# A recurrent attention chain and the linear attention behind it: order of the last attention, and of the hand-over between the two

## The chip, the cores and the metric

The kernel runs on one core of a Trainium2 chip. The metric is the device time of one execution in microseconds (us); the time of a kernel is the median of its timed runs. A separate execution is recorded by the hardware profiler, instruction by instruction, and all rows shown below come from such executions. Engines are called PE (TensorE matmul), PEld (TensorE weight load), DVE (VectorE), ACT (ScalarE), POOL (GpSimd) and SP (SyncE, which here only issues DMAs). A name such as L1049 is a line of the kernel.

## The reference

The input has 2048 rows of 640 numbers in bf16. Four layers are applied, A, B, A, B, each as `x = x + layer(layernorm(x))`.

Layer A is recurrent. The rows are cut into 64 segments of 32, and 8 memory rows are carried from segment to segment:

```
for s in range(64):
    h = concat([mem, xs])                       # 8 + 32 rows
    q, k, v = h @ Wq, h @ Wk, h @ Wv            # 32 heads of 192
    p = softmax(mask(q k^T / sqrt(192)))
    o = (p v) @ Wo
    mem = o[:8]; outs.append(o[8:])
```

A segment can't begin before the 8 memory rows of the one before it are known.

Layer B is a linear attention with 32 heads of 20. For q and k it makes the features `[softmax(x w_phi), softmax(-x w_phi)]`, sums `kv = phi_k^T v` and `z = sum(phi_k)` over all rows, and returns `(phi_q kv) / (phi_q z + 1e-6) @ wo`.

## The kernel before

**The chain of layer A** (`A_chain`). The chain projects the 8 memory rows and 24 of a segment's 32 own rows. The keys, queries and values of the last 8 rows are made ahead for all segments (`A_pre`) and fetched segment by segment (`extra_kq`, `extra_v`); their scores and outputs are made in the chain with the others. The 32 heads are worked in four rounds of eight. The rounds run upwards in even segments and downwards in odd ones, so that weights which are still in the local memory are used again; the others are loaded anew each time by SP.

In a round the chain projects Q and K (L972), copies and transposes them (L982, L987, L990 to L992), adds the extra columns on GpSimd (L948 to L951), makes masked scores (L1009, L1014), weights E by `exp` (`weigh`, L1067), their sums (`sums`, L1081) and the normalised weights (`normalise`, L1086 to L1088), projects V (L972), and applies the weights (`attend`, L1022). The output product W with `Wo` (`wo_round`, L1049) is written as 12 steps for each round, each with four products in 32-column tiles of TensorE. Software writes the order of all engines out by hand inside the chain (`manual_schedule`, L908), one instruction stream per engine, in which no instruction passes another. At the end of a segment the order on TensorE is: steps 0 to 3 of the second round's `wo_round`, last scores, steps 4 and 5, third attention, steps 6 and 7, sums of the last round, steps 8 to 11, the third round's `wo_round`, a few products that only keep TensorE occupied (`keep_busy`, L1056), fourth attention, the fourth `wo_round`, more such products. VectorE then transposes W (L1195, L1196) into the next segment's memory columns.

**Stored outputs.** The attention outputs of the last 8 rows of each segment (columns 64 to 80 of the accumulators `ps_o`) aren't multiplied with `Wo` in the chain. `keep_tail` (L1035, L1037, L1038) copies them into `otb`, which has two buffers, and `store_tail` (L1042, on GpSimd's queue) stores them into a DRAM tensor `otb_d`, one store per round, 512 in the kernel.

**The hand-over to layer B** (`post_steps`, and the part of `layer_B` from L485 on). The stored outputs are brought back in four groups of 16 segments: `fetch` (L1210, SP's queue) loads a group, `spread` reorders it by four copies (L87 on VectorE, L89 on ScalarE), and `multiply` makes 48 pairs of products with `Wo` (L1228, L1229), evicts them (L1231, L1232) and stores them beside the chain's rows. In the first layer B, 32 steps that multiply two weight matrices into one (`fuse`: L166, L393) are called between the pairs of the third and fourth group. `norm_rows` (L352) adds the attention's rows to x (L356, GpSimd) and normalises them (L222 to L244); `turn_rows` (L361) transposes them. The arena of local memory is used by both layers, so a load of layer B waits for the last reader of layer A.

Outside `manual_schedule` a planner in the software orders the instructions of each engine by the times that it expects; `tc.issue_after(i)` says that what follows is queued behind instruction i on that engine, and adds no wait. The planner may also put instructions of layer B among the last ones of the chain.

**Keys, values and normalisers of layer B.** For each 512 rows, `keys_values` makes exponentials of the keys (L424), their sums and reciprocals (L426, L428), copies the reciprocals into the value tile (L433, GpSimd), multiplies the values with them (L437) and adds up `kv` (L443). After the fourth group, each of the twelve parts of `kv` is masked (L529), and its column of z is copied into two places (L534 to L537).

Of the kernel before, what the change touches and what calls it, by code (L numbers as in the profile page):

```python
# [20 lines left out]
FILL = {0: 86, 2: 78}  # L21
# [94 lines left out]
class Kernel:  # L116
# [131 lines left out]
    def layer_B(self, x_dram, at_dram, xout_dram, xnext_dram, li, bp, post):  # L248
# [42 lines left out]
        with tc.tile_pool(name=f"B{li}_kv", bufs=1, space=bass.MemoryType.PSUM, reuse_waits="tile") as kvp, \  # L291
# [121 lines left out]
            def keys_values(g, xnT):  # L413
                VS = DH * (512 // DH)

# [15 lines left out]
                def values(b, ek, rk):  # L431
                    vr = vrs.next().rearrange("p (s h f) -> p s h f", s=2, h=H)
                    nc.gpsimd.tensor_copy(out=vr[:, :, :, DH], in_=rk[:])  # L433
# [50 lines left out]

            with tc.issue_after(self.last_load.ins):  # L485
                load_rows(0)
            fetch, spread, multiply = post
            ot = [fetch(tb) for tb in range(2)]
            ow = [spread(tb, ot[tb]) for tb in range(2)]
            ot += [fetch(tb) for tb in range(2, 4)]  # L490
            for j in (1, 2, 0):
                src = self.B_wqkv.rearrange("(k p) n -> p k n", p=P) if j == 2 or self.fused_d is None else self.fused_d
                nc.sync.dma_start(out=wqkv[:, :, D * j:D * j + D], in_=src[:, :, D * j:D * j + D])
            multiply(0, ow[0], kv_ps[0], side_bank("ps_post"))
            ow.append(spread(2, ot[2]))
            rows = [norm_rows(b) for b in range(4)]
            multiply(1, ow[1], kv_ps[1], side_bank("ps_post"))
            ow.append(spread(3, ot[3]))
# [4 lines left out]
            multiply(2, ow[2], kv_ps[0], side_bank("ps_post"), side)  # L503
            first_xnT = new_xnT()
            for b in range(4):
                turned = turn_rows(b, rows[b], first_xnT)
            multiply(3, ow[3], kv_ps[1], side_bank("ps_post"), side)
            assert not side
            waiting = None
            for g in range(NG):  # L510
                if g == 0:
                    xnT = first_xnT
                elif g == 1:
                    with tc.issue_after(turned.ins):
                        xnT = norm_T(g)
                else:
                    xnT = norm_T(g)
# [7 lines left out]
            for sg in range(2):  # L525
                for c in range(NC_):
# [4 lines left out]
                    for u in range(2):  # L531
                        z = zm[0:mc, sg, c, 32 * u + HC * c:32 * u + HC * c + nh]
                        if sg == 0:
                            nc.vector.scalar_tensor_tensor(out=z, in0=o[:, :, DH], scalar=1e-6, in1=blk[0:mc, 0:nh], op0=ALU.add,  # L534
                                                           op1=ALU.mult)
                        else:
                            nc.vector.tensor_tensor(out=z, in0=o[:, :, DH], in1=blk[0:mc, 0:nh], op=ALU.mult)  # L537
# [734 lines left out]
```

## Time and profile before

| | us |
|---|---|
| median of the timed runs (three) | 3646.74 |
| lowest and highest of them | 3642.9 and 3680.07 |
| the profiled execution | 3628.7 |
| its span, first to last instruction | 3627.0 |
| chain of the first layer A, about | 140 to 1557 |
| first hand-over, to the first keys | 1557 to 1627 |
| second layer A's chain ends | 3370 |
| second hand-over, to the first keys | 3370 to 3426 |

How the rows are to be read. In a timeline, a row has the start, the duration, the engine, the line, the operation, what it writes and reads, the shapes, how many were merged, and in square brackets how long the engine had stood idle and what ended that. In a list of waits, a row has the engine and the instruction that waited, the instruction it waited for, the sum in us, how often, and the longest. In a table by stretches, a row has the stretch, its length, the busy time of PE, PEld, DVE, ACT and POOL with numbers of instructions, the granted TensorE clock (1 is full), the busy share of the DMA engines and their GB/s. Matmuls are pipelined and their ends are modelled, so the distance of two starts tells more than a duration. The granted clock over the whole span was 0.990.

### The profile page before, as it was taken

The page shows a single profiled execution, that of the slowest core. Times are in us where ns is not written, and L with a number is a line of the kernel's source. Part 1 is how long each engine was busy: PE and PEld are TensorE (multiplying, and loading weights), DVE is VectorE, ACT ScalarE, POOL GpSimd, SP SyncE. Part 2 cuts the span into 40 slices and gives each one's busy share as a digit, 9 for nine tenths or more (in the row PEclk, how much of TensorE's full clock was granted, in tenths as well). Part 3 has the DMA queues.
Part 4 walks back from the last instruction along what each step waited for, and adds up shares of the span by engine and source line. Part 5 has one row for each costly group of instructions (what it writes and reads, how often), then busy time and mean ns, then how long its engine had stood idle before and what let it go on. Part 6 is the DMA issues. An engine that isn't in the chain of part 4 may idle for free.

```text
span 3627.0 us, 168472 instructions
## 1 busy us (share of the span) xinstructions
PE 3484.6 (96%) x70944; PEld 2279.2 (63%) x71398; DVE 2332.7 (64%) x6336; ACT 2040.4 (56%) x5233; POOL 1598.2 (44%) x4181
## 2 busy tenths in 40 slices
PE   9989999999999999989999899999999999999899
PEld 7756666666666666655367566666666666666453
DVE  5556666666666666646643566766666676766465
ACT  3356666666566656645432565666666666666463
POOL 3445555555555555531122455555545555555300
PEclk9999999999999999999999999999999999999999
DMA  9988887888788878870387887888888788888600
GB/s 302 338 286 290 284 290 271 285 293 287 270 283 291 290 271 282 293 228 8 130 270 208 287 291 270 291 292 283 282 288 294 274 292 295 281 286 292 214 1 30
DMA packets 533265, 933.32 MB, mean 257 GB/s; under 512 B 141066, under 2 KB 300442, under 8 KB 532506
## 3 DMA queue, kind: packets, MB, share of 16 engines
q1 hardware_dynamic: 431098, 821.50, 64.3%
q0 software_dynamic: 67744, 87.80, 8.0%
q10 hardware_dynamic: 33664, 13.24, 1.4%
q8 instruction: 557, 9.13, 1.0%
q14 instruction: 202, 1.65, 0.1%
HBM read 852.43 MB, written 73.73 MB: 255 GB/s over the span
## 4 chain that ended last, share of the span: by engine, by line
PE 57%; DMA 19%; DVE 7%; issue 7%; ACT 5%; POOL 3%; PEld 2%; SPq 0%; POOLq 0%; DVEq 0%; ACTq 0%
PE ps_qk L972 17%; DMA arena<-wo_rows 7%; PE ps_w L1049 7%; PE ps_v L972 6%; DMA Vp<-vb 5%; PE ps_o L1022 4%; PE ps_pre L863 3%; DMA arena<-in_A_Wv_dram 3%; PE ps_s L1014 3%; DVE hT L928 2%; PE ps_s L1081 2%; PE ps_s L1009 2%; PE ps_pre L887 2%; PE ps_wo L410 2%; PE ps_idle L1056 1%
## 5 line engine op out<-in xcount | busy, mean ns | idle before, releaser
L972 PEld LDWEIGHTS <-hT 128*32 128x32 bf16 x30720 | 753.5, 96 | 453.5 <-issue 29.5
L972 PE MATMUL ps_qk<-arena,hT 128*32 128x384 bf16 x20480 | 998.6, 327 | 11.2 <-DMA arena<-in_A_Wq_dram 2.2
L982 ACT ACTIVATE raw<-ps_qk 128x384 bf16<-128x384 f32 x1024 | 503.2, 491 | 377.0 <-PE ps_s L1081 250.7
L955 POOL DMA_DIRECT2D Vp<-vb x512 | 259.2, 506 | 629.6 <-PE ps_o L1022 467.1
L972 PE MATMUL ps_v<-arena,hT 128*32 128x384 bf16 x10240 | 515.6, 328 | 15.7 <-DMA arena<-in_A_Wv_dram 15.1
L1049 PE MATMUL ps_w<-arena,OT 128*32 128x160 bf16 x18432 | 471.3, 235 | 16.0 <-DMA arena<-wo_rows 15.0
L987 DVE STREAM_TRANSPOSE KT<-raw 128x384 bf16<-128x384 bf16 x512 | 296.1, 578 | 192.1 <-ACT raw L982 188.2
L1049 PEld LDWEIGHTS <-OT 128*32 128x32 bf16 x18432 | 321.1, 96 | 116.5 <-issue 23.6
L990 DVE STREAM_TRANSPOSE QT<-raw 128x256 bf16<-128x256 bf16 x512 | 227.9, 445 | 238.3 <-ACT raw L982 196.5
L943 POOL DMA_DIRECT2D kqb<-kqb x512 | 292.1, 571 | 174.0 <-POOL KT L951 147.0
L1003 DVE CAST Vp<-ps_v 64x384 bf16<-64x384 f32 x512 | 286.1, 559 | 107.3 <-ACT Vp L1001 95.7
L1088 DVE TENSOR_TENSOR E<-E,ps_s 80x320 bf16<-80x320 bf16 x512 | 247.3, 483 | 164.6 <-ACT ps_s L1087 164.2
L1042 POOL DMA_DIRECT2D otb<-otb x512 | 283.9, 554 | 129.6 <-DVE otb L1038 110.8
L1001 ACT ACTIVATE Vp<-ps_v 64x384 bf16<-64x384 f32 x512 | 245.2, 479 | 128.4 <-PE ps_v L972 128.3
L1067 ACT ACTIVATE E<-ps_s 80x320 bf16<-80x320 f32 x512 | 221.9, 433 | 84.8 <-PE ps_s L1014 43.7
L1022 PEld LDWEIGHTS <-Vp 80*128 80x128 bf16 x4096 | 183.5, 99 | 128.1 <-issue 80.2
L1022 PE MATMUL ps_o<-E,Vp 80*128 80x80 bf16 x4096 | 235.6, 203 | 26.3 <-DMA Vp<-vb 10.9
L1014 PE MATMUL ps_s<-QT,KT 128*80 128x80 bf16 (+1 forms) x3072 | 234.0, 213 | 12.4 <-DVE KT L987 10.6
L936 ACT ACTIVATE Vp<-ps_w 32x160 bf16<-32x160 f32 x512 | 150.8, 295 | 167.6 <-DVE wt L1195 154.0
L1086 ACT ACTIVATE ps_s<-ps_s 80x320 f32<-80x320 f32 x512 | 215.3, 420 | 41.6 <-PE ps_s L1081 41.6
L948 POOL COPY QT<-kqb 128x64 bf16<-128x64 bf16 x512 | 125.4, 245 | 252.6 <-PE ps_s L1014 244.7
L1014 PEld LDWEIGHTS <-KT 128*80 128x80 bf16 x3072 | 201.9, 119 | 39.1 <-issue 30.4
(155 smaller groups left out, 5453.8 us busy)
## 6 DMA issues: line engine op xcount, KB each, us to landing
arena<-wo_rows SPq DMA_DIRECT2D x792, 320.0 KB, 6.8
arena<-in_A_Wq_dram SPq DMA_DIRECT2D x427, 384.0 KB, 4.5
arena<-in_A_Wv_dram SPq DMA_DIRECT2D x427, 384.0 KB, 6.4
arena<-in_A_Wk_dram SPq DMA_DIRECT2D x768, 192.0 KB, 4.8
kqb<-kqb POOLq DMA_DIRECT2D x512, 48.0 KB, 5.1
arena<-in_A_Wk_dram SPq DMA_DIRECT2D x43, 384.0 KB, 6.8
vb<-arena POOLq DMA_DIRECT2D x128, 112.0 KB, 5.9
Vp<-vb POOLq DMA_DIRECT2D x512, 28.0 KB, 4.8
```

What stands on the lines that cost most here:

```text
L943: nc.gpsimd.dma_start(out=kqb[:], in_=self.kqb_d[s, :, r, :])
L955: nc.gpsimd.dma_start(out=Vs[n % 2][64:80, :], in_=self.vb_d[s, r].rearrange("g t f -> (g t) f"))
L972: nc.tensor.matmul(o[32 * g:32 * g + 32, 0:384], lhsT=hT[:, b, :], rhs=rhs, start=(i == 0), stop=(i == KC - 1), tile_position=(0, 32 * g), ...
L982: nc.scalar.activation(out=raw[:], in_=ps[:, 0:384], func=ACT.Copy)
L987: nc.vector.transpose(out=KT[:, :, 0:64], in_=raw[:, :].rearrange("p (c j) -> p c j", j=64))
L1001: nc.scalar.activation(out=o, in_=i, func=ACT.Copy)
L1003: nc.vector.tensor_copy(out=o, in_=i)
L1014: nc.tensor.matmul(S[0:80, c0:c0 + 80 * (q1 - q0)], lhsT=KT[:, 3 * x + i, :], rhs=QT[:, x, q0:q1, :], start=False, stop=(x == 1 and i == 2 ...
L1022: nc.tensor.matmul(O[x][:, 80 * i:80 * i + 80], lhsT=Vs[n % 2][0:80, 448 * x + k:448 * x + k + 128], rhs=E[0:80, 160 * x + 80 * e:160 * x ...
L1042: nc.gpsimd.dma_start(out=self.otb_d[s, :, 96 * r:96 * r + 96], in_=otb[:, :, :].rearrange("p c t -> p (c t)"))
L1049: nc.tensor.matmul(W[32 * g:32 * g + 32, 0:160], lhsT=OT[:, c, q:q + 32], rhs=w[:, 640 * i + 160 * g:640 * i + 160 * g + 160], start=(firs ...
L1088: nc.vector.tensor_tensor(out=E[0:80, 0:320], in0=E[0:80, 0:320], in1=rc, op=ALU.mult)
```

## The change

It has six parts.

1. In each segment of the chain, the third attention comes right behind the last scores. Steps 4 and 5 of the earlier `wo_round` move behind it, and steps 6 to 11 all come behind the sums.
2. `otb_d` gets the partition as its outermost dimension: a store writes 192 B in each of 128 places 48 KB apart, and a fetch reads 12 KB from each in place of sixteen times 768 B.
3. The first two groups' fetches are issued in the chain's last segment, one before and one behind the load of the last output weights; the first group is spread there too, behind the fourth attention, by two copies on VectorE and two on ScalarE. The second group's copies are queued behind the chain's last copies on their engines.
4. Keys' and queries' weights of layer B are loaded ahead of x's rows and of the values' weights. The weight products move from the third and fourth group's products to the second and third's. The first four layer norms are queued on VectorE and ScalarE behind the third group's eviction, and their transposes go between the products of the fourth group.
5. The reciprocals of the first 512 rows are copied by VectorE; GpSimd copies the others as before.
6. The column of z is written to its two places by one instruction in place of two: 12 in place of 24 in each layer B. One more filling weight load (79 in place of 78) stands at the second chain's start.

```diff
-FILL = {0: 86, 2: 78}
+FILL = {0: 86, 2: 79}
...
-                    nc.gpsimd.tensor_copy(out=vr[:, :, :, DH], in_=rk[:])
+                    (nc.gpsimd if g else nc.vector).tensor_copy(out=vr[:, :, :, DH], in_=rk[:])
...
+            fetch, spread, multiply = post
+            ot, ow = self.first_tails
             with tc.issue_after(self.last_load.ins):
+                for j in (1, 0):
+                    src = self.B_wqkv.rearrange("(k p) n -> p k n", p=P) if self.fused_d is None else self.fused_d
+                    last = nc.sync.dma_start(out=wqkv[:, :, D * j:D * j + D], in_=src[:, :, D * j:D * j + D])
+            with tc.issue_after(last.ins):
                 load_rows(0)
-            fetch, spread, multiply = post
-            ot = [fetch(tb) for tb in range(2)]
-            ow = [spread(tb, ot[tb]) for tb in range(2)]
+            with tc.issue_after(self.chain_end[0].ins), tc.issue_after(self.chain_end[1].ins):
+                ow.append(spread(1, ot[1]))
             ot += [fetch(tb) for tb in range(2, 4)]
-            for j in (1, 2, 0):
-                src = self.B_wqkv.rearrange("(k p) n -> p k n", p=P) if j == 2 or self.fused_d is None else self.fused_d
-                nc.sync.dma_start(out=wqkv[:, :, D * j:D * j + D], in_=src[:, :, D * j:D * j + D])
-            multiply(0, ow[0], kv_ps[0], side_bank("ps_post"))
+            with tc.issue_after(last.ins):
+                nc.sync.dma_start(out=wqkv[:, :, 2 * D:3 * D],
+                                  in_=self.B_wqkv.rearrange("(k p) n -> p k n", p=P)[:, :, 2 * D:3 * D])
+            multiply(0, ow[0], kv_ps[0], side_bank("ps_post"), {})
             ow.append(spread(2, ot[2]))
-            rows = [norm_rows(b) for b in range(4)]
-            multiply(1, ow[1], kv_ps[1], side_bank("ps_post"))
-            ow.append(spread(3, ot[3]))
             side = []
             if self.fused_d is None:
                 self.fused_d = self.dram.tile([P, KC, 2 * D], BF16, name="fused")
                 side = fuse(1) + fuse(0)
-            multiply(2, ow[2], kv_ps[0], side_bank("ps_post"), side)
+            between = [{3 * i + 2: f for i, f in enumerate(part)} for part in (side[:16], side[16:])]
+            multiply(1, ow[1], kv_ps[1], side_bank("ps_post"), between[0])
+            ow.append(spread(3, ot[3]))
+            done = multiply(2, ow[2], kv_ps[0], side_bank("ps_post"), between[1])
+            with tc.issue_after(done[0].ins), tc.issue_after(done[1].ins):
+                rows = [norm_rows(b) for b in range(4)]
             first_xnT = new_xnT()
-            for b in range(4):
-                turned = turn_rows(b, rows[b], first_xnT)
-            multiply(3, ow[3], kv_ps[1], side_bank("ps_post"), side)
+            turned = []
+            multiply(3, ow[3], kv_ps[1], side_bank("ps_post"),
+                     {35 + 4 * b: lambda b=b: turned.append(turn_rows(b, rows[b], first_xnT)) for b in range(4)})
...
-                    with tc.issue_after(turned.ins):
+                    with tc.issue_after(turned[-1].ins):
...
-                    for u in range(2):
-                        z = zm[0:mc, sg, c, 32 * u + HC * c:32 * u + HC * c + nh]
...
+                    z = zm[0:mc, sg, c, :].rearrange("p (u h) -> p u h", u=2)[:, :, HC * c:HC * c + nh]
+                    zs, own = bcast_mid(o[:, :, DH], 2), bcast_mid(blk[0:mc, 0:nh], 2)
...
-        self.otb_d = dram.tile([NSEG, P, 384], BF16, name=f"otb{li}")
+        self.otb_d = dram.tile([P, NSEG, 384], BF16, name=f"otb{li}")
...
                             if s == NSEG - 1:
+                                tails = [self.fetch_tails(0, low)]
                                 load_wo(3, low[:, 0:7680])
+                                tails.append(self.fetch_tails(1, low))
...
                 S, E = weigh(True)
-                wo_round(W, order[L - 2], OT1, False, False, range(4, 6))
                 OT, o = attend(Ep, L - 1, KT[:, :, 0:64])
...
-                wo_round(W, order[L - 2], OT1, False, False, range(6, 8))
+                wo_round(W, order[L - 2], OT1, False, False, range(4, 6))
                 sums(S, E)
-                wo_round(W, order[L - 2], OT1, False, False, range(8, 12))
+                wo_round(W, order[L - 2], OT1, False, False, range(6, 12))
...
                 OT, o = attend(E, L)
                 tails_after(L)
+                if s == NSEG - 1:
+                    self.first_tails = tails, [self.spread_tails(0, tails[0], low, "vvss")]
...
+    def fetch_tails(self, tb, low):
+        o = 7680 + 12288 * (tb % 2)
+        ot = low[:, o:o + 6144].rearrange("p (s f) -> p s f", f=384)
+        self.nc.sync.dma_start(out=ot, in_=self.otb_d[:, 16 * tb:16 * tb + 16, :])
+        return ot
+
+    def spread_tails(self, tb, ot, low, engines="vsvs"):
+        o = 7680 + 12288 * (tb % 2)
+        ow = low[:, o + 6144:o + 12288].rearrange("p (c q) -> p c q", q=P)
+        for k in range(4):
+            self.ev.copy(out=ow[:, 12 * k:12 * k + 12, :].rearrange("p c (s t) -> p c s t", t=8),
+                         in_=ot[:, :, 96 * k:96 * k + 96].rearrange("p s (c t) -> p c s t", t=8), eng=engines[k])
+        return ow
```

`chain_end` holds the chain's last copy on VectorE (of `keep_tail`) and on ScalarE (of `keep_rows`).

## The prediction

> **What bounds the kernel now.** I read the busy shares first, then TensorE's waits in the two stretches where an attention layer hands over to a linear layer, then the timeline of those stretches, then one ordinary segment.
>
> ```profile
> PE 3484.6 (96%) x70944; PEld 2279.2 (63%) x71398; DVE 2332.7 (64%) x6336; ACT 2040.4 (56%) x5233; POOL 1598.2 (44%) x4181
> ```
>
> TensorE is busy 96% of the span, so only two things can shorten the run: its idle time (3627.0 - 3484.6 = 142 us), and stretches in which it runs slowly. TensorE's waits from 1540 to 1700 us, the first handover:
>
> ```profile
> PE ps_s L1014 <- DVE KT L987: 5.1, 1, 5.1
> PE ps_f L393 <- ACT arena L89: 4.1, 2, 2.9
> PE kv L443 <- POOL arena L433: 3.5, 1, 3.5
> PE ps_v L410 <- ACT arena L424: 2.4, 3, 1.1
> PE ps_f L393 <- DVE arena L87: 1.3, 1, 1.3
> ```
>
> The second handover (3340 us on) has the first again with 5.6 us, the third with 3.5, and neither `ps_f` row, since the weight products are made once. Where the first wait comes from, in the timeline:
>
> ```profile
> 1536.78 0.38 SPq L1210 DMA_DIRECT2D arena<-otb  x1
> ...
> 1548.40 0.56 DVE L87 COPY arena<-arena 128x1536 bf16<-128x1536 bf16 x1 [5.23 <-issue]
> ...
> 1548.88 0.57 DVE L987 STREAM_TRANSPOSE KT<-raw 128x384 bf16<-128x384 bf16 x1
> ...
> 1549.59 0.72 PE L1014 MATMUL ps_s<-QT,KT 128*80 128x80 bf16 x6 [5.09 <-DVE KT L987]
> ```
>
> The copy L87 is the first spreading copy of the linear layer. The planner queued it on VectorE ahead of the K transpose that the last segment's last scores need; its fetch (L1210), issued at 1536.78, has landed only at 1548.4. The chain stands still behind it. What that does to the clock (each row of this table by stretches ends with granted clock, DMA share and GB/s):
>
> ```profile
> 1545.00:1550.00 5.00, 0.41 (x5) 0.44 (x6) 1.49 (x3) 1.57 (x2) 3.79 (x6) 0.89 1.06 362
> 1550.00:1555.00 5.00, 4.90 (x101) 3.64 (x100) 2.20 (x6) 3.27 (x7) 0.58 (x1) 0.50 1.06 348
> ```
>
> After 5 us without work the clock is 0.50 in the next 5. The DMA engines are full (1.06), which matters below.
>
> **The change, part by part.**
>
> *Spreading of the first stored outputs at a fixed place.* It now stands behind the last attention. The chain's stop goes: 5.1 and 5.6 us. With it goes the slow clock: from the scores to the segment's end takes 7.9 us (1549.6 to 1557.5) and 7.5 us (3362.9 to 3370.4), against 5.8 in an ordinary segment (1011.0 to 1017.3 less a DMA wait of 0.5), so 2.1 and 1.7. Together 7.2 and 7.3. What is late next is the fetch itself. It is now queued behind the six loads of the last output weights. From 1538.8 us, the first of those loads: 6 x 0.33 = 1.97 MB, then 1.57 MB of outputs, and some 0.6 MB still in flight, 4.1 MB at the 355 GB/s of the two rows above: 11.7 us, and about 1 for the last piece to be told, so 1551.5; the first copy (0.56) ends at 1552.1. The chain without its stop ends 5.8 us after 1544.6, at 1550.4. TensorE then waits 1.7 us: the gain is 1557.5 - 1552.2 = 5.3; 3370.4 - 3365 = 5.4 at the second. Both ends: 3 (an SP queue that stops) and 7.2 (the transfer is in time, since 128 pieces of 12 KB may move quicker than 2048 of 768 B). I take 5.3: it follows from rows.
> ScalarE's two spreading copies (1.48 each) now stand ahead of its last keep_tail and keep_rows copies. Nothing on the path waits for those: their rows are needed by the fourth fetch, 30 us later. Without that cover (if the first product's accumulator still held the last outputs) it would cost 3 us per handover, contained in the low end.
>
> *Order of SP's queue.* Two fetches, then keys' and queries' weights, then rows, then the other fetches, then the values' weights. No instruction of SP issues faster or slower; bytes are the same 13 MB in 40 us. The second fetch lands at about 1561 (another 3.5 MB), while the first product runs to 1565 (48 x 0.272 = 13.1 us by the rows of L1228/L1229): hidden. The third lands near 1571 and is needed at 1582: hidden for itself, but see the first rival.
>
> *Weight products in the second and third product instead of the third and fourth; layer norms behind them.* The waits of the `ps_f` rows, 4.1 + 1.3 = 5.4 us, come from evictions queued behind the norms of the first rows; both engines have no norms in front of them now. Once only. New: the same evictions can be queued behind the third spreading, which waits for its fetch. Ends 0 and 4 us; I take 1.5, since five transposes and four banks run ahead of it. The norms start when the third product is evicted. Chain of a row block from the timeline: 0.9 statistics, 0.4 moments, 0.5 ScalarE, 0.3 VectorE, 0.9 apply: 3 us, next blocks 1.4 apart, and the first transposition comes 35 x 0.272 = 9.5 us into the last product: hidden. In the second layer 0.9 + 0.7 us of waits (`ps_x`, `ps_post`) go. Norms of the next 512 rows (6 us VectorE, 6 us ScalarE) move under the first key blocks, where each has about a third free.
>
> *The reciprocals' copy on VectorE for the first 512 rows.*
>
> ```profile
> 1635.24 2.74 POOL L356 TENSOR_TENSOR arena<-arena 128x640 bf16<-128x640 bf16 x2 [5.80 <-DMA arena<-attn]
> 1637.93 0.46 POOL L433 CAST arena<-rk 128x64 bf16<-128x64 f32 x1
> ...
> 1638.44 0.58 PE L443 MATMUL kv<-arena 128*120 128x126 bf16 x4 [3.53 <-POOL arena L433]
> ```
>
> The copy stands behind 2.74 us of additions on GpSimd. VectorE's products were there from 1634.8: 3.5 us go, and the clock of 0.55 in 1640 to 1645 (5 x 0.45 = 2.2). Against that four copies on VectorE of some 0.15 to 0.2 each (nearest row: a 128x48 cast, 0.2) and the norms that moved here. Ends 2 and 6 per layer; I take 4.
>
> *Twelve normaliser steps fewer.* 24 of 0.1 us in each layer are 12; TensorE waits for none of them (0.5 us of other waits there). Zero; ends 0 and 1.
>
> *Third attention right behind the last scores, 128 times.* An ordinary segment:
>
> ```profile
> 2364.51 0.48 DVE L1088 TENSOR_TENSOR E<-E,ps_s 80x320 bf16<-80x320 bf16 x1 [0.18 <-ACT ps_s L1087]
> 2364.52 0.45 PE L1014 MATMUL ps_s<-QT,KT 128*80 128x80 bf16 x6
> 2364.90 0.12 PEld L1049 LDWEIGHTS <-OT 128*32 128x32 bf16 x8
> ...
> 2365.16 0.46 PE L1022 MATMUL ps_o<-E,Vp 80*128 80x80 bf16 x8
> ...
> 2365.80 0.33 PE L1081 MATMUL ps_s<-E,ones_blk 80*80 80x320 bf16 x1
> ```
>
> Eight output products (L1049, 32-column tiles) lie between scores and attention. The last score starts at 2364.77, so they cost 0.38 there; placed with the others of their kind they cost 2 x 0.07. The Trainium skill (TensorEngine Tiling (Array Packing), Key Properties) says that changing the tiling mode drains TensorE; one pair of changes disappears. By that rule alone a segment gets 0.38 - 0.04 - 0.14 = 0.20 shorter, 26 us in 128. The rows say otherwise: the third attention's weights E end at 2364.99, so it can start only 0.05 later, at 2365.04 instead of 2365.16, and TensorE idles 0.23 there. The sums come 0.12 earlier, the two moved steps are then in the way again, and the fourth attention can start 0.09 earlier where it waits for its own E. Over the 128 segments of the trace that is so in 33 (the fourth attention starts within 0.075 of E's end); in the rest a transfer of V rows lands later and the gain is lost there. 33 x 0.09 = 3 us; ends 0 and 11 (all 128).
>
> *Stored outputs with the partition outermost.* Each store is still 128 pieces of 192 B, now 48 KB apart. The skill (DMA: Bandwidth & Descriptors, Latency and other measured facts) warns of large row pitches in HBM: 207 GB/s at 512 KB, about half at 4 MB. It speaks against the change, but the trace's loads of Wq have a pitch of 60 KB and bring 384 KB in 4.5 us; a pitch below 512 KB in the rule and near 60 KB in the trace: zero. The other end is the third rival.
>
> **Sum**, against the profiled execution (3628.7 us; span 3627.0): first handover 5.3 + 5.4 - 1.5 + 4 = 13.2, second 5.4 + 1.6 + 4 = 11.0, chain 3: 27 us, giving 3601 there. The timed runs' median is 3646.74, 18 above that execution; the difference is not the change's, so 3646.7 - 27 = 3620.
>
> **Rivals.**
> - *The waits come back in another place* (0.22): SP stops between the loads, the first product waits 3 us more, evictions wait behind the third spreading. Gain 12 to 18: 3631. For it: DMA full from 1540 to 1580. Against it: the bytes fit.
> - *The drain rule holds in full* (0.08), because E comes earlier than I read: 3620 - 23 = 3597. Against it: E's end sits 0.22 behind the last score in most segments.
> - *The tail stores get slow* (0.09), on the other side. Two buffers of `otb` are in turn; ScalarE already waits for the older store:
>
> ```profile
> ACT Vp L936 <- DVE wt L1195: 154.0, 123, 2.3
> ACT otb L1037 <- DMA otb<-otb: 87.9, 110, 1.7
> ```
>
>  Behind that copy ScalarE has 1.25 us to spare (154.0/123). A store takes 4.7 us in the median; from 6 on every further us is paid 128 times. At 6.4: 0.45 x 128 = 58, less 27: 3678; at 7, 3750.
> - *The fetch is not freed* (0.08): if the new layout makes the first fetch wait for the latest stores, the chain's later stores queue behind it, some 10 us a layer: 3640.
> My forecast, 3604 to 3632, has 0.53.
>
> **How the numbers follow.** 3599 to 3648 holds the forecast, the first, the fourth and part of the second. One per cent, 36 us, is about what a measurement of this kernel can tell from no change. Faster by more: 0.22 (the second rival, the forecast's lower edge and the unknown ends up together). Slower by more: 0.07 of the third. The rest is within.
>
> **What would show it.** Right: no wait of L1014 for L987 at the handovers; the first product some 5 us earlier after a short wait for the spreading; no `ps_f` wait of over 1 us; no wait of `kv` for GpSimd; the clock not at 0.50 after the chain; in a segment a TensorE gap of 0.2 ahead of the third attention. Wrong: L1037 or L1035 waiting longer for stores, an eviction of `ps_t` queued behind a spreading copy, or a segment period that moved by over 0.1 us.

## The result, and the profile after

The changed kernel took 3619.61 us in the median of nine runs (3614.55 to 3631.28), the kernel before 3645.82 beside it: a ratio of 0.9922, 95% interval 0.9894 to 0.995, 26.2 us less. On a second chip it was 3601.32 against 3627.89, 0.9918 (0.9898 to 0.9938), 26.6 us less. The profiled execution took 3619.27 us, its span was 3617.5.

Lines have moved: the scores are now L1019, the attention L1027, `wo_round` L1054, the sums L1086, the weights E L1093, the fetch L1213, the first of each pair of products L1243, `keep_tail` on ScalarE L1042, the reciprocals' copy L432, `kv` L442. The busy shares of the page of after:

```profile
PE 3470.1 (96%) x70978; PEld 2278.5 (63%) x71399; DVE 2329.5 (64%) x6320; ACT 2030.9 (56%) x5233; POOL 1592.2 (44%) x4173
```

TensorE's waits from 1525 to 1660 us, the first hand-over (sum, how often, longest):

```profile
PE kv L1243 <- DVE arena L87: 3.8, 1, 3.8
PE ps_v L410 <- ACT arena L423: 3.0, 3, 1.3
PE kv L442 <- DVE arena L436: 1.4, 2, 0.9
PE ps_w L1054 <- issue: 0.3, 1, 0.3
```

Three of the old rows are gone: the scores' wait for the K transpose (5.1), both waits of `ps_f` (5.4) and the wait of `kv` for GpSimd (3.5). One is new: the first product waits 3.8 us for the first spreading copy, and 4.6 at the second hand-over. Where it comes from, in the timeline:

```profile
1538.97 0.32 SPq L1213 DMA_DIRECT2D arena<-otb  x1
1539.35 5.15 SPq L687 DMA_DIRECT2D arena<-wo_rows  x6
...
1544.44 1.15 PE L1054 MATMUL ps_w<-arena,OT 128*32 128x160 bf16 x48
...
1549.40 1.03 DVE L87 COPY arena<-arena 128x1536 bf16<-128x1536 bf16 x2 [4.99 <-DMA arena<-otb]
...
1550.02 0.61 PE L1243 MATMUL kv<-arena 128*128 128x512 bf16 x1 [3.83 <-DVE arena L87]
```

The fetch, issued at 1538.97, lands 10.4 us later. The chain's last product has ended at 1545.6, and behind a few filling products TensorE has nothing else to do. In the table by stretches the clock behind that wait is 0.69, and 0.56 at the second hand-over (third number from the end), and each pair of products takes 0.53 us in place of 0.27:

```profile
1545.00:1550.00 5.00, 1.19 (x33) 0.78 (x23) 0.60 (x2) 0.54 (x1) 0.38 (x1) 0.97 1.00 333
1550.00:1555.00 5.00, 4.98 (x25) 2.52 (x26) 0.54 (x2) 3.59 (x7) 1.15 (x2) 0.69 1.07 420
...
3365.00:3370.00 5.00, 2.44 (x9) 1.17 (x10) 1.14 (x3) 3.03 (x4) 0.00 (x0) 0.56 1.06 402
```

The trace places the slow clock more closely. It is 0.50 from 1549.7 for 3.4 us and from 3365.6 for 6.8 us. In before it is 0.50 for 6.8 us at the end of each of the four stops (two at the scores, two at `kv`): from 1548.9, 1637.7, 3361.4 and 3436.5.

An ordinary segment now, in the timeline:

```profile
2352.29 0.48 DVE L1093 TENSOR_TENSOR E<-E,ps_s 80x320 bf16<-80x320 bf16 x1 [0.18 <-ACT ps_s L1092]
2352.29 0.45 PE L1019 MATMUL ps_s<-QT,KT 128*80 128x80 bf16 x6
...
2352.82 0.45 PE L1027 MATMUL ps_o<-E,Vp 80*128 80x80 bf16 x8
2353.20 0.32 PE L1054 MATMUL ps_w<-arena,OT 128*32 128x160 bf16 x8
2353.45 0.33 PE L1086 MATMUL ps_s<-E,ones_blk 80*80 80x320 bf16 x1
```

The third attention starts 0.05 behind the end of its weights E. Over 126 segments it starts, in the median, 0.271 us behind the start of the last score (before: 0.384), the last sums 0.900 (1.027). But the distance of two segments (last sums to last sums) has a median of 21.20 us, and 21.15 before; the second profiles have 21.12 and 21.10. TensorE's waits over the whole run show where the 0.1 us went. Before, and then after:

```profile
PE ps_w L1049 <- DMA arena<-wo_rows: 15.0, 25, 4.2
PE ps_w L1049 <- issue: 11.7, 30, 0.9
```

```profile
PE ps_w L1054 <- DMA arena<-wo_rows: 25.3, 52, 6.2
...
PE ps_w L1054 <- issue: 17.4, 32, 1.4
```

The stores of the tails have not changed: they land 4.8 us after their issue (4.7 before). ScalarE waits longer for them, 103.7 us in place of 87.9, which was to be a sign of being wrong. It is not the layout's: the second profiles have 97.6 and 95.4, and the run e1 below, with the old layout, has 105.4.

Stage by stage, two profiles of each kernel say more than one. The second profile of before comes from the run `e0_before_again`, that of after from `e10_after_again`. All times count from the last sums of the chain's last segment but one, so that the length of the chain falls out; us.

| up to | before, 2 profiles | after, 2 profiles | mean gain |
|---|---|---|---|
| first hand-over: first product | 33.2, 31.8 | 29.9, 30.3 | 2.4 |
| first keys | 102.8, 102.5 | 95.4, 94.4 | 7.7 |
| last `kv` | 215.7, 214.8 | 204.5, 203.5 | 11.2 |
| second chain's first sums | 475.6, 477.7 | 467.1, 467.1 | 9.5 |
| second hand-over: first product | 33.2, 33.0 | 31.5, 29.4 | 2.6 |
| first keys | 88.1, 92.4 | 87.8, 85.0 | 3.9 |
| last `kv` | 202.3, 203.9 | 196.7, 194.0 | 7.8 |
| end | 289.4, 289.4 | 281.5, 278.8 | 9.2 |

The hand-overs give 9.5 + 9.2 = 18.7 us, though two profiles of one kernel differ by up to 4.3 us at a mark. The runs e1 and e2 below, one with the old hand-overs and one with the new, bear it out: the last `kv` comes at 215.8 and 200.9 in e1, at 205.8 and 193.4 in e2. The chains between these marks give nothing: 2687.2 and 2680.0 before, 2694.1 and 2680.4 after.

### The profile page after: what moved, and what is told of

Its sections match the earlier page's. It is cut to its first block, busy times and chain, and to the rows that moved or that the text cites. A ratio compares the mean times of both kernels' runs of the same rounds, so it can differ in the third digit from the quotient of the medians.

```text
span 3617.5 us, 168478 instructions
## 1 busy us (share of the span) xinstructions
PE 3470.1 (96%) x70978; PEld 2278.5 (63%) x71399; DVE 2329.5 (64%) x6320; ACT 2030.9 (56%) x5233; POOL 1592.2 (44%) x4173
## 4 chain that ended last, share of the span: by engine, by line
PE 59%; DMA 23%; DVE 6%; ACT 6%; issue 4%; POOL 2%; SPq 0%; POOLq 0%; ACTq 0%; DVEq 0%
PE ps_qk L977 17%; DMA arena<-wo_rows 12%; PE ps_w L1054 6%; PE ps_v L977 5%; DMA arena<-in_A_Wv_dram 5%; PE ps_pre L867 5%; PE ps_o L1027 3%; PE ps_s L1019 3%; PE ps_pre L891 2%; PE ps_s L1086 2%; PE kv L1243 2%; DVE E L1093 2%; DMA Vp<-vb 2%; ACT raw L987 2%; DVE hT L932 2%
## 5 line engine op out<-in xcount | busy, mean ns | idle before, releaser
L1054 PE MATMUL ps_w<-arena,OT 128*32 128x160 bf16 x18432 | 451.7, 235 | 26.1 <-DMA arena<-wo_rows 25.3
L1054 PEld LDWEIGHTS <-OT 128*32 128x32 bf16 x18432 | 324.7, 96 | 118.5 <-issue 40.8
L1093 DVE TENSOR_TENSOR E<-E,ps_s 80x320 bf16<-80x320 bf16 x512 | 247.3, 483 | 151.6 <-ACT ps_s L1092 150.5
L1027 PEld LDWEIGHTS <-Vp 80*128 80x128 bf16 x4096 | 188.9, 98 | 120.6 <-issue 95.3
L1027 PE MATMUL ps_o<-E,Vp 80*128 80x80 bf16 x4096 | 232.7, 201 | 29.0 <-DMA Vp<-vb 7.5
L1019 PE MATMUL ps_s<-QT,KT 128*80 128x80 bf16 (+1 forms) x3072 | 233.2, 213 | 1.8 <-POOL KT L956 1.7
L1033 ACT ACTIVATE OT<-ps_o 128x192 bf16<-128x192 f32 x384 | 125.4, 327 | 169.3 <-PE ps_o L1027 169.3
```

The lines of the kernel that those rows point to most:

```text
L1019: nc.tensor.matmul(S[0:80, c0:c0 + 80 * (q1 - q0)], lhsT=KT[:, 3 * x + i, :], rhs=QT[:, x, q0:q1, :], start=False, stop=(x == 1 and i == 2 ...
L1027: nc.tensor.matmul(O[x][:, 80 * i:80 * i + 80], lhsT=Vs[n % 2][0:80, 448 * x + k:448 * x + k + 128], rhs=E[0:80, 160 * x + 80 * e:160 * x ...
L1054: nc.tensor.matmul(W[32 * g:32 * g + 32, 0:160], lhsT=OT[:, c, q:q + 32], rhs=w[:, 640 * i + 160 * g:640 * i + 160 * g + 160], start=(firs ...
L1093: nc.vector.tensor_tensor(out=E[0:80, 0:320], in0=E[0:80, 0:320], in1=rc, op=ALU.mult)
```

## The experiments

Each group of four kernels ran on one chip with the kernel before beside it. The medians of before were 3644.5, 3627.6 and 3627.9 us; differences below are to the before of the same chip.

**First group: the parts apart.** Order of the last attention alone, in the kernel before:

```diff
-                wo_round(W, order[L - 2], OT1, False, False, range(4, 6))
                 OT, o = attend(Ep, L - 1, KT[:, :, 0:64])
...
-                wo_round(W, order[L - 2], OT1, False, False, range(6, 8))
+                wo_round(W, order[L - 2], OT1, False, False, range(4, 6))
                 sums(S, E)
-                wo_round(W, order[L - 2], OT1, False, False, range(8, 12))
+                wo_round(W, order[L - 2], OT1, False, False, range(6, 12))
```

> The kernel before with the chain's new order alone (third attention right behind the last scores). Theory of the prediction: 3 us faster than before (ratio 0.999), since TensorE then waits 0.23 us for the third attention's weights and most segments wait for a transfer at the fourth attention. Rival 1, the drain rule in full: 0.20 us x 128 = 26 us faster (0.993). Rival 2, from the profile of the changed kernel, whose first chain is 4.5 us shorter: some 9 us faster in both chains (0.9975). The stop of 5 us at each hand-over stays in all three.

3645.17 against 3644.49, ratio 1.0003 (0.9987 to 1.0018): between 4.7 us faster and 6.6 slower. The 3 us lie inside; a gain of 26 us, of a drain saved in every segment, does not, nor do the 9 of the second rival.

The changed kernel with the old order:

```diff
+                wo_round(W, order[L - 2], OT1, False, False, range(4, 6))
                 OT, o = attend(Ep, L - 1, KT[:, :, 0:64])
...
-                wo_round(W, order[L - 2], OT1, False, False, range(4, 6))
+                wo_round(W, order[L - 2], OT1, False, False, range(6, 8))
                 sums(S, E)
-                wo_round(W, order[L - 2], OT1, False, False, range(6, 12))
+                wo_round(W, order[L - 2], OT1, False, False, range(8, 12))
```

> The changed kernel with the chain's old order. Theory of the prediction: 24 us faster than before (ratio 0.9934). Rival, from the profiles: the spreading is waited for 3.8 and 4.6 us with a slow clock behind it, so the two hand-overs bring 16 us together (0.9956). From the last segment's scores to the first keys: 75 us before at the first hand-over; 62 by the theory, 66 by the rival.

3619.76, ratio 0.9935 (0.9915 to 0.9954), 24.7 us less. So the hand-over carries the gain, the order none that can be told. From the last segment's scores to the first keys it takes 76.5 us, neither 62 nor 66, and 77.9 and 78.2 in before: the stop lies ahead of these scores, so this distance could not show it. The two kernels say something more. The granted clock of each run gives the time lost to a slow clock, one less the clock, times the span: 45.3 us in the mean of the runs of e1 and 44.5 for before, 32.0 here.

The changed kernel with the stored outputs in their old layout:

```diff
-        self.otb_d = dram.tile([P, NSEG, 384], BF16, name=f"otb{li}")
+        self.otb_d = dram.tile([NSEG, P, 384], BF16, name=f"otb{li}")
```

> The changed kernel with the segment outermost in the stored outputs again (stores 768 B apart, fetches in 2048 pieces of 768 B). Theory of the prediction (the 48 KB pitch costs nothing): stores land in the same 4.7 to 4.8 us, chain the same within 5 us, and the fetches take up to 2 us longer, so the first product starts 0 to 2 us later at each hand-over: 0 to 4 us slower than the changed kernel. Rival (the pitch slows the stores): ScalarE's waits for the stores (103.7 us in the changed kernel) fall to 88 or less and the run is 5 to 15 us faster than the changed kernel.

3624.21, 0.9948 (0.9929 to 0.9966). Against the changed kernel's 0.9918 and 0.9922 on other chips that is some 10 us slower, against e2 on the same chip 4.5 us, both with intervals that overlap. The trace shows less: stores land in 4.8 us in both layouts, and ScalarE waits 97.9 us for them, not 88. The eight fetches land in 12.8 us in place of 10.7, the first product waits 4.9 and 4.3 us, and from the last segment but one to the second chain it is 470.7, 3.6 more. The layout costs nothing at the stores; by the fetch it may be worth a few us, which the runs don't settle.

The changed kernel with all reciprocals copied by GpSimd:

```diff
-                    (nc.gpsimd if g else nc.vector).tensor_copy(out=vr[:, :, :, DH], in_=rk[:])
+                    nc.gpsimd.tensor_copy(out=vr[:, :, :, DH], in_=rk[:])
```

> The changed kernel with the reciprocals of the first 512 rows copied by GpSimd again. Theory of the prediction: the wait of 3.5 us ahead of the first kv product and a slow clock come back in each layer, 4 us each, 8 us slower than the changed kernel. Rival (GpSimd's additions now lie elsewhere, since the norms moved): no wait of over 1 us and no difference in time.

3623.81, 0.9943 (0.9924 to 0.9962). TensorE's waits in its first hand-over, two rows:

```profile
PE kv L442 <- DVE arena L436: 0.9, 1, 0.9
PE kv L442 <- POOL arena L432: 0.7, 1, 0.7
```

The wait for GpSimd is 0.7 (1.5 at the second hand-over), not 3.5. From the first keys to the first `kv` it is 10.3 us at both hand-overs, against 9.1 to 9.4 in the two profiles of after: the copy's move is worth 1.1 us a layer. By time the kernel is some 8 us slower than the changed one on other chips and 4 us slower than e2 on the same chip, with intervals that overlap, so the time can't tell the theory's 8 us from these 2. The rest of the old wait goes with the other parts; which of them was not tried. And the copy isn't cheap on VectorE; in after's timeline:

```profile
1623.21 1.10 DVE L432 CAST arena<-rk 128x64 bf16<-128x64 f32 x1
...
1627.13 0.29 DVE L432 CAST arena<-rk 128x64 bf16<-128x64 f32 x1
```

**Second group: what is left at the hand-over, and the gap ahead of the third attention.** The first fetch a round earlier:

```diff
                     to_rows(q_or_k("K", n + 1), "K")
+                    if n == 0 and s == NSEG - 1:
+                        tails = [self.fetch_tails(0, low)]
...
-                                tails = [self.fetch_tails(0, low)]
```

> The changed kernel with one edit: in the last segment the first fetch is issued behind the second K projection's copies, one round earlier, so ahead of the six loads of the third group's weights instead of behind them. Theory (TensorE's wait for the first spreading copy, 3.8 and 4.6 us, is the six loads of 0.33 MB ahead of the fetch in the same DMA engines): the fetch lands about 6 us earlier, the wait falls below 1 us at both hand-overs, the slow clock behind it goes (0.56 to 0.76 for 5 to 10 us), and the time falls by 8 to 12 us: 3608 to 3612. Rival (the DMA engines are simply full, and what is put first delays the rest): the last output products wait for their weights instead, and the time is 3616 to 3624, the wait of the first product shorter but one at the weights' place as long.

3611.06 against 3627.57, 0.9947 (0.9928 to 0.9967): no faster than the changed kernel on the other chips, by the ratios some 10 us slower. Its timeline:

```profile
1527.75 0.33 SPq L1214 DMA_DIRECT2D arena<-otb  x1
...
1539.41 1.03 DVE L87 COPY arena<-arena 128x1536 bf16<-128x1536 bf16 x2
...
1541.37 0.32 PE L1054 MATMUL ps_w<-arena,OT 128*32 128x160 bf16 x8 [0.73 <-DMA arena<-wo_rows]
1542.32 0.32 PE L1054 MATMUL ps_w<-arena,OT 128*32 128x160 bf16 x8 [0.64 <-DMA arena<-wo_rows]
1543.58 0.32 PE L1054 MATMUL ps_w<-arena,OT 128*32 128x160 bf16 x8 [0.94 <-DMA arena<-wo_rows]
```

The fetch is there in time and the wait for the spreading is gone, but the last `wo_round` now waits five times, 3.1 us, for its weights. Counted as in the table, the first product starts at 30.4 us (after: 29.9 and 30.3). The rival held: the DMA engines are full (share 1.03 from 1525 to 1545), and what goes first delays the rest.

The weight products back in the third and fourth product, with the rows' transposes behind the fourth:

```diff
-            multiply(1, ow[1], kv_ps[1], side_bank("ps_post"), between[0])
+            multiply(1, ow[1], kv_ps[1], side_bank("ps_post"), {})
...
-            done = multiply(2, ow[2], kv_ps[0], side_bank("ps_post"), between[1])
+            done = multiply(2, ow[2], kv_ps[0], side_bank("ps_post"), between[0])
...
-                     {35 + 4 * b: lambda b=b: turned.append(turn_rows(b, rows[b], first_xnT)) for b in range(4)})
+                     between[1])
+            for b in range(4):
+                turned.append(turn_rows(b, rows[b], first_xnT))
```

> The changed kernel with one edit: the 32 weight products stand in the third and fourth product again, and the row transposes behind the fourth. First layer only. Theory (the prediction's step): the waits of ps_f for evictions behind the norms, 5.4 us, come back in part, less the wait for the third spreading (none in the trace of after): 4 to 6 us slower than the changed kernel, 3624 to 3626, and ps_f rows of over 1 us in the first hand-over. Rival (the waits came from the norms being queued ahead of them, and these are now queued behind the third product's eviction wherever the weight products are): no ps_f wait in the third product, one in the fourth at most, under 2 us: 3618 to 3623.

3615.41, 0.9966 (0.9949 to 0.9983), slower than the changed kernel by some 17 us where 4 to 6 were expected. Not by the expected wait, though: no `ps_f` row of a microsecond came back, and from the first product to the first keys it takes 65.6 us (65.5 and 64.0 in after). So the place of the weight products is not what took the 5.4 us away. The rival's cause is left, the layer norms that now stand behind the third group's eviction; no run moves the norms alone. What the kernel loses comes later: 379.0 us from the first keys to the second chain's first sums, against 371.7 and 372.8. This kernel moves the transposes as well, and those in both layers, not in the first only, so that it mixes two causes. The second layer has no weight products and tells them apart: from the first keys to the end it takes 198.4 us, against 193.7 and 193.8, and these 4.6 us are the transposes' alone. A row of TensorE's waits in the first layer points to them too (the second has it with 1.6 us):

```profile
PE ps_x L166 <- ACT arena L244: 1.8, 2, 1.3
```

The profile has some 12 of the 17 us (9 up to the second chain, 3 behind it). From the first keys to the last `kv` TensorE waits 9.8 and 8.4 us in the two layers, in place of 5.0 and 4.8 in after; the rest is not settled.

The third attention with a constant in place of E:

```diff
-                OT, o = attend(Ep, L - 1, KT[:, :, 0:64])
+                OT, o = attend(wo_mid[:, 0:320], L - 1, KT[:, :, 0:64])
```

> The changed kernel with one edit: the third attention of each segment takes its left operand from a constant stretch of the output weights, in place of its own weights E. The multiplication with the third round's own weights is left out; all other instructions stay. TensorE's wait of 0.23 us ahead of the third attention goes. Theory (the fourth attention starts when a transfer of V rows has landed, in nine segments of ten, so what is won before it is lost there): the gap ahead of the third attention falls from 0.27 to about 0.04, the wait ahead of the fourth grows by as much, and the time is within 5 us of the changed kernel, 3614 to 3622. Rival (the segment's length is the sum of TensorE's steps): 0.23 x 128 = 29 us less, 3590.

3665.83 against 3627.57, ratio 1.01 (1.0076 to 1.0124): 38 us *slower*, which no theory had. The gap was gone (the attention starts 0.035 behind the last score), but one row of TensorE's waits over the whole run had grown from 17.4 us, and the timeline shows such a wait in the middle of the dense output products:

```profile
PE ps_w L1054 <- issue: 68.2, 103, 2.6
```

```profile
2407.16 0.66 PE L1054 MATMUL ps_w<-arena,OT 128*32 128x160 bf16 x27
2408.39 0.59 PE L1054 MATMUL ps_w<-arena,OT 128*32 128x160 bf16 x21 [0.57 <-issue]
```

"Issue" is a wait that no semaphore ends. I counted TensorE's records between the first sums of two segments: 1024 in every kernel so far, in all 126 segments, and 1025 here, because the edit gives one weight load a second wait, which takes an instruction of its own. In the other kernels nearly all of these waits fall on one instruction, the 581st behind the first sums, in the last `wo_round`; here they wander. The page's list of DMA queues has one that carries instructions (packets, MB, share of the engines):

```profile
q8 instruction: 557, 9.13, 1.0%
```

That is 16.4 KB a packet; 557 packets for some 142,600 records of TensorE are 256 each. And of the waits put down to issue, the middle eight in ten end 1.26 to 1.55 us after the end of such a packet, in this kernel as in after.

The kernel before once more, unedited:

> The kernel before without any edit, for a second profile: the first one's execution, 3628.7, was lower than every timed run of that kernel (3632.8 to 3680). Theory (the 17 us between it and the median are slow clock and slow segments, drawn anew in each execution): a span of 3635 to 3655, the same stops at both hand-overs (5 us at the scores, 3.5 at the first kv, 4 to 5 at ps_f), and the difference to the first profile in the lost clock (36 us there, one less the granted clock times the span) and in the length of the chains. Rival (the difference is a wait that the first profile did not show): a row of over 5 us in the waits that the first profile lacks.

3623.53 us, again below before's median there (3627.57). The same stops, in TensorE's waits of the first hand-over:

```profile
PE ps_s L1014 <- DVE KT L987: 4.7, 1, 4.7
PE ps_f L393 <- ACT arena L89: 4.1, 2, 3.1
PE kv L443 <- POOL arena L433: 3.6, 1, 3.6
```

The expected span of 3635 to 3655 was missed: this chip is 17 us faster. No new wait is in it. Its time lost to the clock is 36 us, as in the first profile of before; over the timed runs of that kernel the mean is 45.9 on this chip.

**Third group: one instruction, and lighter transfers.** The changed kernel again, as the mark:

> The changed kernel without any edit, as the mark for the other kernels of this chip and as a second profile of it. Theory (the gain belongs to the hand-overs, in every execution): 0.992 to 0.995 of the kernel before, 18 to 29 us; in the profile no wait of the scores for the K transpose, no ps_f wait, and the wait of the first product for the spreading copy, 3.5 to 5 us at both hand-overs. Rival (the first comparison had a lucky draw): a ratio of 0.996 or more.

3601.32, 0.9918 (0.9898 to 0.9938), with the stages of the table above. The first product waits 1.8 and 4.0 us, the first of them less than expected.

The kernel with the constant, and one filling weight load less in each segment:

```diff
-SEG_FILL = 2
+SEG_FILL = 1
```

> The third attention reads a constant in place of its weights E, as in the run before (the multiplication with the third round's own weights is left out), and each segment has one filling weight load less, 1 in place of 2. In the run before, that edit gave the third attention's first weight load a second wait, which costs one more TensorE instruction: its segments have 1025 instructions in the trace where all others have 1024, four times 256. Theory (TensorE's waits with no releaser are the fetch of its next 256 instructions; with 1025 the border moves through the segment into the dense output products): with 1024 again the waits put down to issue fall from 68 us to under 20, all at one place of the segment, and the time falls by 35 to 55 us, to within 8 us of the changed kernel. Rival (the edit itself is slow, by the reading of the constant or the earlier attention): it stays 35 us or more slower than the changed kernel. On the gap of 0.23 us ahead of the third attention: if transfers set the segment's length, the time is within 5 us of the changed kernel; if TensorE's own steps do, it is 20 to 29 us faster.

3608.26: 57 us less than with 1025 instructions (on another chip, whose before is within 0.4 us), 7 us more than the mark. There are 1024 records in a segment again, and the waits for issue are at one place, though not under the 20 us expected. TensorE's waits over the whole run:

```profile
PE ps_w L1054 <- issue: 25.1, 44, 1.4
PE ps_o L1027 <- DMA Vp<-vb: 23.0, 50, 1.7
```

This answers both questions. One instruction a segment was what made the kernel slow. And the gap ahead of the third attention is worth nothing here: it is gone in 97 segments of a hundred, 0.17 us each in the mean, and the fourth attention starts 0.65 us behind the end of its own E in the median where it was 0.35. The mark has 12.9 us for the first row and 7.9 for the second.

Half of the last round's weight loads left out, in the changed kernel:

```diff
-                            load_wo(order[L])
+                            load_wo(order[L], part=range(6) if s in (0, NSEG - 1) else range(3))
```

> The changed kernel with only three of the six weight loads (L687) of the last round's output weights in 126 of 128 segments: half of these weights are left as they were, so the products use old ones. 0.98 MB of each segment's transfers go, of some 6 MB. Theory (the chain's length is set by transfers: weights, V rows and instruction fetches share the DMA engines): DMA share in the chain from about 0.8 to 0.7, the waits for wo_rows nearly gone (25 us), those for V rows and issue down by half or more, and the time 30 to 60 us below the changed kernel. Rival (TensorE's and the other engines' steps set it): within 10 us of the changed kernel.

3555.12, 46 us below the mark. TensorE's waits over the whole run:

```profile
PE ps_w L1054 <- DMA arena<-wo_rows: 9.1, 7, 4.9
...
PE ps_w L1054 <- issue: 1.8, 7, 0.4
```

These were 21.7 and 12.9 in the mark; the wait for V rows, 7.9 there, is gone, and the DMA share inside the chains falls from 0.82 to 0.71. So the loads, and what queues among them, do set the chain's length. The same with the old order of the third attention:

> The same light loads with the order of the third attention as before, and all of the hand-over's changes: it differs from the run before it by the order alone. Theory (the order gains 0.09 us where the fourth attention waits for its own E, in 33 to 56 of 126 segments under full loads, in nearly all when the transfers are light): the order of before is 6 to 12 us slower than the new one under light loads, while under full loads the difference was nil. Rival (the gain of 0.09 goes elsewhere, to steps that no transfer sets): the two are within 3 us of each other.

3573.99, 19 us slower, the ratios 0.9797 (0.978 to 0.9813) and 0.9842 (0.9822 to 0.9863). Only here does the order count. Its size is not settled: the median distance of two segments is 20.69 with the old order and 20.59 with the new, 0.10 us as expected and 12.5 in 126 segments, but the mean distances (20.83 and 20.81) and the spans of these two profiles (2.5 us apart) hardly differ. The old order's profile was the fastest of its four executions by 12 us. The fourth attention waits for its own E in 103 of 126 segments with the old order and light loads, in 33, 46 and 56 with the old order and full loads.

## Why the prediction was right, and where it was not

3620 was forecast and 3619.6 measured, but the sum behind it has errors that cancel, so that a hit this close is in part luck. Most parts of the change did what was said of them; some sizes and the last step were wrong.

- **The chain's stop, 5.3 + 5.4 predicted: 2.4 + 2.6 measured** up to the first product. The stop went as said; "what is late next is the fetch itself" was right too, and the wait for it was mis-sized: 3.8 and 4.6 us (1.8 and 4.0 in the second profile) in place of 1.7. Counted from the last segment but one, the first chain ends about where I put it or later (25.5 and 28.0 us against 25.7), and the fetch lands 2.4 and 2.9 us later than the sum of bytes gave. The 1 us "for the last piece to be told" is not what was too small: from the end of the last packet to the copy it takes 0.7 us (1548.74 to 1549.40). The bytes were: that sum had 4.1 MB, and the packets of after show 5.6 MB between the issue of the first load (1534.5) and the landing. Of these, 0.8 MB belong to the six loads that were issued behind the fetch. A fetch ends in sixteen parts, from 1546.6 to 1549.4, and some of what stands behind it in the queue moves before the last part is there. The first rival had such a wait, and the stop brings some 3 us less at each hand-over, as it said; the waits behind the third spreading that it also had did not come. The clock falls to 0.50 again behind the wait, where "the clock not at 0.50 after the chain" was to be the sign.
- **Weight products and norms, 5.4 - 1.5 + 1.6 predicted: 5.4 and 1.3 measured** from first product to first keys. TensorE waits for no eviction behind a spreading copy. The working named the right queue; e9 shows that the place of the weight products is not what counts, and leaves that of the norms.
- **Reciprocals' copy, 4 + 4 predicted: 3.4 and 3.8 measured** from the first keys to the last `kv`. Right in size and wrong in cause: the copy itself gives 1.1 a layer (e4) and takes up to 1.10 us on VectorE, where I had 0.15 to 0.2; the rest came with other parts.
- **Third attention, 3 predicted: -6.6 to 4.7 measured.** The rows were read rightly (attention 0.11 earlier, sums 0.13, fourth attention 0.10 where the transfers are light), and so was the reason that most of it is lost: under full loads e1 and e2 can't tell the order, under light ones e7 and e8 can. Even the third of the segments in which E was last gave nothing: with 0.1 us less in front of them the weights' and V rows' transfers were more often last there too (the fourth attention starts within 0.08 us of E's end in 33 and 46 segments before, in 24 and 20 after). A gain of 26 us from the drain rule (the Trainium skill, TensorEngine Tiling (Array Packing), Key Properties) is excluded by e1. The drain itself is not: in e5, where the attention doesn't wait for E, the sums come 0.31 us earlier, and without the 0.14 of the two steps that moved behind them 0.17 is left, by this estimate near the 0.20 that the prediction worked out. So the rule's size may hold, hidden by the wait for E and by the transfers.
- **Layout: zero predicted at the stores, and zero it is.** The rival with slow stores fell: 4.8 us to landing. The warning of the Trainium skill about large row pitches (DMA: Bandwidth & Descriptors, Latency and other measured facts) has no counterpart here at 48 KB.
- **The step that failed** is the last: "The timed runs' median is 3646.74, 18 above that execution; the difference is not the change's". The 27 us were worked out for profiled executions, and there the two kernels differ by 14.6 us only (3628.7 and 3623.5 against 3619.3 and 3603.8); the timed runs differ by 26. So part of the difference between timed and profiled runs of before is the change's. Time lost to the clock, from the granted clock of the runs, mean for each kernel:

| hand-over | kernels | us lost to the clock |
|---|---|---|
| as before | before on three chips, e1 | 44.5, 45.9, 43.2, 45.3 |
| as after | after on two chips, e2, e3, e4, e6, e9 | 29.8, 28.2, 32.0, 31.1, 32.6, 33.3, 33.7 |

So 12 to 15 us of the gain are clock (e2 and after, each against its own before), if every us lost makes the run as much longer, and 11 to 14 are left for waits. It may be less: in the four profiles three quarters of the loss fall on time in which TensorE works. My sum had 24 of waits with the clock's share in it, of which 3.8 at the chain's end and 2.2 at `kv` were named as clock. The two profiles of before had lost only 36 us, against 43 to 46 in its timed runs, while after lost 29 in its profiles and 28 to 30 in its timed runs: that is 7 to 10 of the 12 us by which the timed gain is larger than the profiled one. In the profiles the two hand-overs together, each up to its last `kv`, lose 14 and 17 us before and 5 and 3 after. Where the timed runs lose the others is open: the profile of e1 (3666 us, 61 lost) has 22 of them in the first linear layer behind the last `kv`, with the clock at 0.50 for 27 us and no wait over 0.7 us ahead of it; one profile is no rule.

## What to carry to other kernels

What a shortened step gives is decided by what ends last after it: where transfers end last, 0.1 and 0.2 us a segment on TensorE vanished whole, and the 0.1 showed once the transfers were lighter. A stop of TensorE can cost more than its length: at the end of each stop of before began 6.8 us at half clock. So compare the granted clocks of the timed runs, not of one profile, before calling a difference between them chance. An experiment that changes the number of TensorE's instructions in a loop may measure that alone: count them first.

## What was not expected

TensorE's instructions are themselves a load. The runs show 256 of them to a packet of the instruction queue, a restart 1.26 to 1.55 us after such a packet, and a loop of 1024 instructions in which only one border of four is felt: 13 to 17 us in 126 segments of after, 1.8 with lighter loads. With 1025 the border moves through the loop, the waits are 68 us, and the kernel takes 57 us longer than with 1024. The Trainium skill (Runtime: NRT & Kernel Launch, Instruction fetch mechanics) has the same 256 instructions in 16 KiB and calls the cost of a border mostly hidden; in the dense output products, beside DMA engines with a share of 0.82, it is not. This also gives the two fillers a meaning that the prediction had none for. With `SEG_FILL` at 2 a segment has 1024 instructions. And with the one more filling load at the second chain's start, the first sums of both chains stand at the same place modulo 256 in the records of after as in the second profile of before (125).
